# A new order of products and vector work in a fused convolution and SwiGLU kernel

## The chip, the cores and the metric

The kernel runs on one core of a Trainium2 chip. The metric is the time of one execution on the device in microseconds (us). A core has a matrix engine (TensorE, PE in the profile, which writes only to the eight banks of PSUM), a vector engine (VectorE, DVE), a scalar engine (ScalarE, ACT), GpSimd (POOL, which works on SBUF only here) and SyncE (SP), which issues the DMAs. Each engine takes its instructions in the order of the program, and waits where one needs what another engine has not finished yet.

## The reference

The input x has 8 sequences of 4096 tokens of 192 channels. First comes a causal convolution of 7 taps in each channel, with taps that are a softmax over the 7 weights of the channel's head (8 heads of 24 channels):

```python
w = np.exp(weight - np.max(weight, axis=-1, keepdims=True))
w = w / (np.sum(w, axis=-1, keepdims=True) + 1e-09)
out = np.einsum('hk,bskhg->bshg', w, x_unf)      # x_unf: the 7 last tokens of each token
```

Then a SwiGLU block without bias on all 32768 tokens, with d_ff = 1536:

```python
rms = np.sqrt(np.mean(x * x, axis=-1, keepdims=True) + 1e-06)
xn = x / rms * rms_g
g = xn @ w_gate
silu = g * (1.0 / (1.0 + np.exp(-g)))
val = xn @ w_val
return (silu * val @ w_out).astype(np.float32)
```

## The kernel before, in words

**Pairs.** The tokens are worked on in 32 "pairs" of 1024 tokens, that is two groups of 512. Pair 0 is done in a plain way and overlaps the start of the kernel. Pairs 1 to 31 run through the class `Pair` (L821) and take nearly all of the time. A pair has two stages on TensorE: a product stage, which makes gate and value and from them the hidden activations, and an output stage, which multiplies these with w_out.

**Product stage.** The 1536 hidden columns are cut into 4 units of 3 x 128. A unit is a block product: 2 groups of tokens, 3 blocks of inner length 64 (192 = 3 x 64) and 3 blocks of columns, so 6 outputs, numbered v = 0 to 5. In place of 18 block products it makes 15, of sums of inputs (`XSUM`, made once a pair) and sums of weights (`WSUM`, made once). The 15 results are added up in PSUM so that most serve several outputs. `CHAIN` (L713) lists them in order as (v, i): product i is added to the bank that stands for v. `product` (L746) issues one; every product is issued twice, for half 0 (the gate, partitions 0 to 63) and half 1 (the value, partitions 64 to 127). The two halves run side by side in the matrix engine, and every matmul in fp32 leaves two records in the trace. A half has four PSUM banks, handed out from a list of free ones (`free`, `pick`).

**Vector steps.** `Unit.do` (L754) has the steps that go with the products. A name such as `AS41.0.1` in `ORDER` is: the engine (V = VectorE, A = ScalarE, G = GpSimd), the step, the half and the unit.
- S copies a bank to a tile in SBUF (S40, S41, S42, S44: four states of bank 4, as it grows; S00 and S51: banks 0 and 5).
- F ("fork") copies a bank into a new one, from which another output goes on: `FORK` (L717) says that output 0 starts from bank 1, output 2 from bank 4 and output 3 from the negative of bank 5. The fork of bank 4, F2, is made in two parts: F2a, columns 0 to 319 on ScalarE, then F2b, columns 320 to 511 on VectorE (`CUT`, L720).
- C, D and R add a snapshot to a bank, or take it off; R also ends an output and frees its bank. G is the silu of the gate, M the product with the value; G4 and M4 free bank 4.

**Output stage.** It makes a two-by-two block product with seven products in place of eight (`OUTS`), in 84 steps of `tile` (L879). Its sums of activations (S1 to S4 followed by a block number; names with one number after the point) are GpSimd's. In the same time the vector engines prepare later pairs: `cv` are the taps of the convolution for the pair after next, `sq`, `red`, `pow`, `bc`, `mul` its norm, `X0` to `X10` the sums of inputs for the next pair (X10 is the last to touch the input that the next pair's second product (1,4) reads), `fetA`, `fetB`, `load`, `place` and `st` are DMAs, and C22, C21, T22, T21, T12, T11 the last sums and transposes of the output.

**What sets the order.** `ORDER` (L90) is a table that stands in the program. "p2" means: issue two steps of TensorE's line. Everything else is issued where it stands, and a trailing "-" says that the step belongs to the pair before. The order within each engine is therefore that of the table, and where a step stands against the "p" entries also decides which value of a bank it sees, and so who waits for whom. TensorE's own line comes from `products` (L857). Products of a unit before: (4,11), (1,4), (5,6), (4,9), (0,8), (5,13), (4,5), (1,10), (0,3), (4,7), (5,2), (4,12), (2,1), (3,14), (4,0). A product on bank 4 must wait until the snapshot or the fork of the state before it has been read.

Of the kernel before, what the change touches and what calls it, by code (L numbers as in the profile page):

```python
# [19 lines left out]
def kernel(  # L20
# [22 lines left out]
    T = 512  # L43
# [9 lines left out]
    NU = FC // NF  # L53
# [34 lines left out]

    SPAN = 1509
    ORDER = (  # L90
        "p2 Dst1- VT11- p2 AS40.1.0 VS40.0.0 p2 AF0.1.0 GX7- AF0.0.0 Dst0- p2 VC.0.0 Dload-",
        "GX4- p2 VC.1.0 AS41.0.0 VS41.1.0 p2 AS00.1.0 AS00.0.0 p2 VD5.1.0 p2 Vbc- VD5.0.0",
        "AS42.0.0 Gmul- AS42.1.0 p2 AS51.1.0 VR1.1.0 AS51.0.0 p2 VR1.0.0 p2 AF2a.0.0 VF2b.0.0",
        "AF2a.1.0 VF2b.1.0 AG1.0.0 VR0.0.0 p2 VR0.1.0 AF3.0.0 p2 VS44.0.0 AF3.1.0 Dplace- p1",
        "AS44.1.0 VR5.0.0 p1 AG0.0.0 VR5.1.0 p1 AG5.0.0 p1 GM0.1.0 VR3.0.0 p1 AG4.0.0 p1",
        "VR3.1.0 AG3.0.0 GM1.1.0 p1 VR2.1.0 p1 AS40.0.1 VR2.0.0 p1 AS40.1.1 GM5.1.0 p1",
        "VM4.1.0 AF0.0.1 p1 AF0.1.1 VC.0.1 p1 AG2.0.0 p1 VC.1.1 p1 AS41.1.1 GM2.1.0 VS41.0.1",
        "p2 VS00.0.1 AS00.1.1 p1 GM3.1.0 VD5.0.1 p2 VD5.1.1 AS42.0.1 p1 GS3.1 AS42.1.1 p1",
        "VR1.0.1 p1 AS51.0.1 AS51.1.1 p1 VR1.1.1 p1 AG1.0.1 VR0.0.1 p1 AF2a.0.1 GM1.1.1 p1",
        "VF2b.0.1 AF2a.1.1 VF2b.1.1 AG0.0.1 p1 VR0.1.1 p1 AF3.0.1 GS3.0 VF3.1.1 p1 AS44.0.1",  # L100
        "p1 AS44.1.1 VR5.0.1 p1 GS1.0 p1 VR5.1.1 AG5.0.1 p2 VR2.0.1 GM0.1.1 p1 VR2.1.1",
        "AG4.0.1 p1 VR3.1.1 AG2.0.1 p1 GM5.1.1 p1 VR3.0.1 AS40.0.2 p1 AS40.1.2 VM4.1.1 p1",
        "GM2.1.1 AF0.0.2 p1 AF0.1.2 VC.0.2 p1 GS3.2 p1 VC.1.2 p1 AS41.1.2 VS41.0.2 p2",
        "VS00.0.2 GS1.2 AS00.1.2 p1 AG3.0.1 p1 VD5.1.2 GM3.1.1 p1 AS42.0.2 p1 VD5.0.2",
        "AS42.1.2 p1 VR1.0.2 p1 AS51.0.2 GS1.1 AS51.1.2 p1 VR1.1.2 p1 AG1.0.2 VR0.0.2 p1",
        "GS2.1 AF2a.0.2 p1 VF2b.0.2 AF2a.1.2 VF2b.1.2 p1 VR0.1.2 AF3.0.2 p1 GS2.0 VF3.1.2 p1",
        "AS44.0.2 p1 AS44.1.2 VR5.0.2 GM1.1.2 p2 VR5.1.2 AG5.0.2 p2 VR2.0.2 AG0.0.2 GM5.1.2",
        "p1 VR2.1.2 AG2.0.2 p1 VR3.1.2 AG4.0.2 p1 GS2.2 p1 AS40.0.3 VR3.0.2 AS40.1.3 p1",
        "VM4.1.2 p1 GM0.1.2 AF0.0.3 p1 AF0.1.3 VC.0.3 p1 AG3.0.2 GS4.2 p1 VC.1.3 p1 AS41.1.3",
        "VS41.0.3 p1 AS00.0.3 GM3.1.2 p1 VS00.1.3 p2 VD5.0.3 GS3.3 p1 VD5.1.3 AS42.0.3 p1",  # L110
        "AS42.1.3 p1 VR1.0.3 p1 AS51.0.3 GS1.3 AS51.1.3 p1 VR1.1.3 p1 AG1.0.3 VR0.1.3 p1",
        "AF2a.0.3 GM1.1.3 p1 VF2b.0.3 AF2a.1.3 VF2b.1.3 p1 VR0.0.3 p1 GM2.1.2 VF3.1.3 AF3.0.3",
        "p2 AS44.0.3 AS44.1.3 p1 VR5.0.3 GS3.4 p1 VR2.0.3 p1 AG5.0.3 p1 VR5.1.3 GS2.3 AG4.0.3",
        "p2 Acv0_2 VM4.1.3 p1 AG0.0.3 p1 VR3.0.3 p1 GS3.5 DfetA p1 VR3.1.3 AG3.0.3 p1 Vcv1_2",
        "p1 Acv0_1 p1 GM3.1.3 AG2.0.3 VR2.1.3 p2 Acv0_0 p2 GS1.4 Ac1 Vcv1_0 p3 VM0.1.3 p2",
        "VM5.1.3 p2 Vcv1_1 p1 GS1.5 p2 Vcv2_1 p2 Vcv2_2 GS2.5 As7 DfetB p2 Vcv2_0 p2 GS2.4",
        "Vcv3_1 p2 Vcv3_2 p2 VX3 p2 GS4.3 Vcv4_1 p2 Vcv5_1 p2 GS4.4 Vcv3_0 p2 Vcv4_2 p1 GS4.0",
        "p1 Ac2 Vcv4_0 p2 Vcv6_1 p1 GM2.1.3 p4 VX0 p1 GS4.5 Vcv5_0 p3 Vcv6_0 p1 GS4.1 p1",
        "Vcv5_2 p3 Vcv6_2 GX9 p2 VC22 Asq p2 VX1 p2 GX2 VT22 p2 Vred p2 GX6 p3 GX5 p1 VC21 p3",
        "VX8 p2 GX10 VT21 p2 VT12 p1 Gpow p3",  # L120
    )

    cst = ctx.enter_context(tc.tile_pool(name="cst", bufs=1))
# [569 lines left out]
    def put(at, do):  # L693
        heapq.heappush(line, (at, next(tick), do))
# [5 lines left out]
    def plus(s):  # L700
        return ALU.add if s > 0 else ALU.subtract
# [3 lines left out]
    def copy(eng, dst, src, s=1):  # L705
        if eng == "A":
            nc.scalar.activation(out=dst, in_=src, func=AF.Copy, scale=float(s))  # L707
        elif s < 0:
            nc.vector.tensor_scalar(out=dst, in0=src, scalar1=-1.0, scalar2=None, op0=ALU.mult)
        else:  # L710
            nc.vector.tensor_copy(out=dst, in_=src)  # L711

    CHAIN = (  # L713
        (4, 11), (1, 4), (5, 6), (4, 9), (0, 8), (5, 13), (4, 5), (1, 10), (0, 3), (4, 7),
        (5, 2), (4, 12), (2, 1), (3, 14), (4, 0),
    )
    FORK = {0: (1, 1), 2: (4, 1), 3: (5, -1)}  # L717
    RESULT = {1: ("42", -1), 0: ("41", -1), 2: ("51", -1), 5: ("44", -1), 3: ("c", 1)}

    CUT = 320  # L720

    class Unit:
        def __init__(self, u):
# [30 lines left out]
        def do(self, eng, act, h):  # L754
            tl, kind, v = self.tl, act[0], int(act[1:2] or 0)
            if kind == "S":
                t = tl[act[1:], h] = tiles.pop(0)
                copy(eng, t[:], self.old(v, h))
            elif kind == "F":
                src, s = FORK[v]  # L760
                cols = {"a": slice(0, CUT), "b": slice(CUT, T)}.get(act[2:], slice(0, T))
                dst = self.old(v, h) if (v, h) in self.bk else self.new(v, h)
                copy(eng, dst[:, cols], self.old(src, h)[:, cols], s)
            elif kind == "D":
                b, t = self.old(5, h), tl.pop(("00", h))
                nc.vector.tensor_tensor(out=b, in0=b, in1=t[:], op=ALU.add)
                tiles.append(t)
            elif kind == "C":
                t = tl["c", h] = tl.pop(("40", h))
                nc.vector.tensor_tensor(out=t[:], in0=self.old(5, h), in1=t[:], op=ALU.add)  # L770
            elif kind == "R":
                k, s = RESULT[v]
                t = tl.pop((k, h))
                nc.vector.tensor_tensor(  # L774
                    out=self.hv(v) if h else t[:], in0=self.old(v, h), in1=t[:], op=plus(s)
                )
                self.leave(v, h)
                if h:
                    tiles.append(t)
                else:  # L780
                    tl["g", v] = t
            elif kind == "G":
                if v in RESULT:
                    t = src = tl["g", v]
                else:
                    t, src = tiles.pop(0), self.old(v, 0)
                nc.scalar.activation(out=t[:], in_=src[:], func=AF.Silu)  # L787
                if v not in RESULT:
                    self.leave(v, 0)
                tl["g", v] = t  # L790
            else:
                t = tl.pop(("g", v))
                src = self.hv(v) if v in RESULT else self.old(v, 1)
                engine[eng].tensor_tensor(out=self.hv(v), in0=src, in1=t[:], op=ALU.mult)  # L794
                if v not in RESULT:
                    self.leave(v, 1)
                tiles.append(t)
# [23 lines left out]
    class Pair:  # L821
# [33 lines left out]
            free[h].append(i)  # L855

        def products(self):  # L857
            for u in self.units:
                for v, i in CHAIN:
                    for h in range(2):  # L860
                        u.product(h, v, i)
                        yield
            for form, b, lo, hi in OUTS:
                first = form in (1, 7)
                if first:
                    self.open(b, False)
                for k in range(lo, hi):
                    src, right = self.left(form, k), RIGHT[form][:, k]
                    fresh = first and k == 0
                    wide = src.rearrange("p (b q e) -> p q b e", q=2, e=Q)  # L870
                    slim = src.rearrange("p (b q e) -> p q b e", q=NQ, e=Q)
                    for i in range(NQ):
                        self.tile(b, i, 0, 2 * P, right[:, i // 2], wide[:, i % 2], fresh)
                    yield
                    for i in range(NQ):
                        self.tile(b, i, 2 * P, P, right[:, 2], slim[:, i], False)
                    yield
# [87 lines left out]
    def plain(hts):  # L965
# [27 lines left out]
        def values():  # L993
            for u, g, f in groups:
# [7 lines left out]
                yield  # L1002

        return products(), silus(), values()

    LAG = 138
# [116 lines left out]
    p, sl, v = plain(hts)  # L1123
# [31 lines left out]
    c = base + 200  # L1155
# [17 lines left out]
    for p in range(1, PAIRS + 1):  # L1173
        now = Pair(p) if p < PAIRS else None
        for w in order:
# [5 lines left out]
            eng, name = w[0], w[1:]  # L1181
# [34 lines left out]
```

## Time and profile before

| | |
|---|---|
| median of 3 runs | 2668.94 us (2662.84 to 2669.16) |
| profiled execution, span | 2663.6 us |
| matmuls of the product stage (L748) | 7440 records |
| matmuls of the output stage (L880) | 20832 records |
| first part of the fork on ScalarE, 128x320 | 248, mean 423 ns |
| second part on VectorE, 128x192 | 248, mean 366 ns |
| whole copy of a bank to a bank on ScalarE, 128x512 | 403, mean 585 ns |
| whole copy of a bank to SBUF on ScalarE, 128x512 | 1209, mean 597 to 598 ns |
| convolution tap on VectorE (L446), bank to bank | 435, mean 749 ns |
| input sums on VectorE (L669), from the inputs alone | 94, mean 1422 ns |

How to read it: the records of the product stage lie two side by side, one for each half, so their durations must not be added up; the distance from one start to the next tells how fast TensorE goes. A matmul's end is modelled, and matmuls overlap, so a share of 99% busy does not mean that nothing is lost. VectorE and ScalarE overlap their instructions a little too: from start to start they take some 0.08 us less than the duration of one. The chain of waits follows the work that ended last backwards, and shows on which engine time passes that nobody else could hide. A window table gives the busy time of each engine in a stretch; the share of the idle rest on an engine which is not the bound costs nothing.

### The profile page before, as it was taken

What the parts mean: (1) busy time and instruction counts of PE and PEld (TensorE: products, weight loads), DVE (VectorE), ACT (ScalarE), POOL (GpSimd) and SP (SyncE); (2) the same over time, 40 slices, a digit from 0 to 9 for tenths busy, and PEclk for the clock granted to TensorE, in tenths of its full rate; (3) what the DMA queues carried; (4) which work ended last, traced back from release to release, by engine and by line L of the source; (5) the groups of instructions that cost most, each with busy time, mean ns of one, the idle gap of its engine ahead of it and who ended that gap; (6) DMA issues with size and microseconds to landing.
All of it is one profiled execution on the core that took longest, in us unless ns stands there. A gap on an engine that the chain in (4) does not pass through costs nothing.

```text
span 2663.6 us, 71444 instructions
## 1 busy us (share of the span) xinstructions
PE 2623.9 (99%) x29002; PEld 1594.7 (60%) x29002; DVE 2321.4 (87%) x3793; ACT 1562.4 (59%) x2933; POOL 2188.7 (82%) x1785
## 2 busy tenths in 40 slices
PE   6999999999999999999999999999999999999999
PEld 4666666566665556565566565665655656655665
DVE  8988889888889888888888898888988888988865
ACT  5365555765556755556655566555566555676554
POOL 3988889887888888897888888888988888888877
PEclk9999999999999999999999999999999999999999
DMA  6312331323312223213233222233132332122210
GB/s 141 59 35 55 62 55 33 62 38 62 62 38 49 49 51 62 55 33 61 38 62 62 43 44 50 50 62 59 33 58 38 62 62 49 38 54 45 49 37 14
DMA packets 510663, 138.05 MB, mean 52 GB/s; under 512 B 482300, under 2 KB 484860, under 8 KB 510205
## 3 DMA queue, kind: packets, MB, share of 16 engines
q1 hardware_dynamic: 509772, 133.44, 26.5%
q8 instruction: 227, 3.72, 0.6%
q14 instruction: 104, 0.85, 0.1%
q10 hardware_dynamic: 560, 0.03, 0.0%
HBM read 83.87 MB, written 49.55 MB: 50 GB/s over the span
## 4 chain that ended last, share of the span: by engine, by line
PE 94%; DVE 2%; POOL 1%; DMA 1%; SPq 1%; issue 1%; ACT 1%; DVEq 0%; POOLq 0%
PE ps L748 61%; PE ps L880 32%; PE ps L979 1%; POOL wf L351 1%; ACT ps L707 0%; DVE ps L711 0%; SPq L219 0%; SPq L1117 0%; DMA x<-in_x_dram 0%; DMA xh<-in_x_dram 0%; POOL wo_sb L313 0%; DMA ht<-in_moe_w_gate_dram 0%; DMA ht<-in_moe_w_val_dram 0%; DVE xc L669 0%; DVE ht L996 0%
## 5 line engine op out<-in xcount | busy, mean ns | idle before, releaser
L748 PE MATMUL ps<-xc,wf 64*128 64x512 f32 x4960 | 1308.4, 596 | 2.6 <-DVE xc L669 0.9
L748 PEld LDWEIGHTS ps<-xc,wf 64*128 64x128 f32 x4960 | 619.2, 186 | 547.8 <-issue 376.2
L748 PE MATMUL ps<-xb,wf 64*128 64x512 f32 x2480 | 738.2, 591 | 0.0
L707 ACT ACTIVATE tile<-ps 128x512 f32<-128x512 f32 (+1 forms) x703 | 396.4, 593 | 339.9 <-PE ps L748 194.6
L707 ACT ACTIVATE tls<-ps 128x512 f32<-128x512 f32 (+1 forms) x568 | 326.0, 592 | 339.3 <-PE ps L748 198.0
L794 POOL TENSOR_TENSOR ht<-ht,tile 128x512 f32<-128x512 f32 x310 | 391.7, 1274 | 110.5 <-ACT tile L787 110.5
L748 PEld LDWEIGHTS ps<-xb,wf 64*128 64x128 f32 x2480 | 319.8, 187 | 232.2 <-issue 192.7
L707 ACT ACTIVATE ps<-ps 128x512 f32<-128x512 f32 x682 | 343.0, 521 | 91.5 <-PE ps L748 25.2
L794 POOL TENSOR_TENSOR ht<-ht,tls 128x512 f32<-128x512 f32 x248 | 314.3, 1274 | 95.8 <-ACT tls L787 95.8
L908 POOL TENSOR_TENSOR early<-ht 128x512 f32<-128x512 f32 x279 | 354.1, 1274 | 34.2 <-DVE ht L794 26.9
L446 DVE SCALAR_TENSOR_TENSOR ps<-xh,tp,ps 128x512 f32<-128x512 f32 x435 | 307.4, 749 | 18.2 <-ACT ps L438 16.2
L880 PE MATMUL ps<-ht,wo_sb 128*32 128x256 f32 (+1 forms) x6944 | 309.9, 326 | 0.0
L908 POOL TENSOR_TENSOR ht<-ht 128x512 f32<-128x512 f32 x186 | 238.4, 1282 | 49.1 <-DVE ht L794 36.9
L880 PEld LDWEIGHTS ps<-ht,wo_sb 128*32 128x32 f32 x6944 | 218.0, 110 | 91.2 <-issue 23.5
L774 DVE TENSOR_TENSOR tile<-ps,tile 128x512 f32<-128x512 f32 x341 | 232.0, 683 | 21.6 <-PE ps L748 10.1
L880 PE MATMUL ps<-ht,x 128*32 128x256 f32 (+1 forms) x5952 | 249.6, 326 | 0.2 <-issue 0.2
L774 DVE TENSOR_TENSOR ht<-ps,tile 128x512 f32<-128x512 f32 x357 | 241.6, 681 | 7.4 <-ACT tile L707 7.4
L880 PEld LDWEIGHTS ps<-ht,x 128*32 128x32 f32 x5952 | 194.4, 110 | 49.6 <-issue 0.3
L787 ACT ACTIVATE tile<-tile 128x512 f32<-128x512 f32 x341 | 212.5, 629 | 17.6 <-DVE tile L774 16.8
L774 DVE TENSOR_TENSOR tls<-ps,tls 128x512 f32<-128x512 f32 x279 | 189.9, 684 | 21.8 <-PE ps L748 10.4
L880 PE MATMUL ps<-early,x 128*32 128x256 f32 (+1 forms) x4464 | 193.9, 326 | 0.0
L774 DVE TENSOR_TENSOR ht<-ps,tls 128x512 f32<-128x512 f32 x263 | 177.9, 681 | 8.2 <-ACT tls L707 8.2
(130 smaller groups left out, 3297.8 us busy)
## 6 DMA issues: line engine op xcount, KB each, us to landing
xb<-xd SPq DMA_DIRECT2D x124, 384.0 KB
xd<-yn SPq DMA_DIRECT2D x248, 96.0 KB
out_dram<-o_sb SPq DMA_DIRECT2D x186, 128.0 KB
xh<-in_x_dram SPq DMA_DIRECT2D x192, 105.0 KB
xh<-in_x_dram SPq DMA_DIRECT2D x56, 98.4 KB
ht<-in_moe_w_gate_dram SPq DMA_DIRECT2D x12, 192.0 KB
ht<-in_moe_w_val_dram SPq DMA_DIRECT2D x12, 192.0 KB
tls<-in_moe_w_out_dram SPq DMA_DIRECT2D x8, 192.0 KB
```

Of the source, the lines that this page charges most:

```text
L351: nc.gpsimd.tensor_tensor(out=t[:, d, :], in0=t[:, a, :], in1=t[:, b, :], op=ALU.add if op == "add" else ALU.subtract,)
L446: nc.vector.scalar_tensor_tensor(out=dst, in0=xk, scalar=w, in1=at, op0=ALU.mult, op1=ALU.add)
L707: nc.scalar.activation(out=dst, in_=src, func=AF.Copy, scale=float(s))
L748: nc.tensor.matmul(out=self.new(v, h, True) if first else self.old(v, h), lhsT=wf[self.u][HALF[h], WAT[i], :], rhs=x_op(XOP[i])[HALF[h]], ...
L774: nc.vector.tensor_tensor(out=self.hv(v) if h else t[:], in0=self.old(v, h), in1=t[:], op=plus(s))
L787: nc.scalar.activation(out=t[:], in_=src[:], func=AF.Silu)
L794: engine[eng].tensor_tensor(out=self.hv(v), in0=src, in1=t[:], op=ALU.mult)
L880: nc.tensor.matmul(out=self.bank(b)[i * Q : (i + 1) * Q, at : at + n], lhsT=left, rhs=cols, start=fresh, stop=True, skip_group_check=True, ...
L908: engine[eng].tensor_tensor(out=dst, in0=a, in1=b, op=op)
L979: nc.tensor.matmul(out=bank(h, bks[h])[:], lhsT=wf[u][HALF[h], k * NF + f, :], rhs=xb[HALF[h], g, k, :], start=(k == 0), stop=(k == KP - 1 ...
```

## The change

There are three parts.

1. The products of neighbouring units are interlaced: the last product of a unit on bank 4, (4,0), is issued after the first product of the next unit, (4,11). (4,9) goes ahead of (5,6), (4,5) ahead of (5,13), (4,7) ahead of (0,3), and (4,12) behind (2,1). It is meant to leave two other products between any two on bank 4, which leaves the snapshot or fork more time. Unit 0 and unit 3 have rows of their own, since unit 0 has no unit before it and unit 3 none after it in the pair.
2. The fork of bank 4 becomes one copy (F2) on ScalarE. `CUT` goes.
3. `ORDER` is written anew for all engines: some snapshots and forks, multiplications and input sums change their engine, and nearly all change their place. X10, X2 and X5 go from GpSimd to VectorE, X1 and X3 the other way; T21 goes from the end of the output stage into unit 0 of the next pair.

```diff
     SPAN = 1509
     ORDER = (
-        "p2 Dst1- VT11- p2 AS40.1.0 VS40.0.0 p2 AF0.1.0 GX7- AF0.0.0 Dst0- p2 VC.0.0 Dload-",
...
-        "AF2a.1.0 VF2b.1.0 AG1.0.0 VR0.0.0 p2 VR0.1.0 AF3.0.0 p2 VS44.0.0 AF3.1.0 Dplace- p1",
...
-        "Vcv5_2 p3 Vcv6_2 GX9 p2 VC22 Asq p2 VX1 p2 GX2 VT22 p2 Vred p2 GX6 p3 GX5 p1 VC21 p3",
-        "VX8 p2 GX10 VT21 p2 VT12 p1 Gpow p3",
+        "p2 VT11- p2 AS40.1.0 AS40.0.0 p2 AF0.0.0 GX9- AF0.1.0 Dst0- p2 VC.1.0 Dload- GX4- p2",
+        "Vbc- AS41.0.0 VS41.1.0 VC.0.0 p1 AS00.1.0 p1 Gmul- VT21- AS00.0.0 p2 AS42.0.0",
...
+        "AS40.0.1 VR5.0.0 AS40.1.1 p2 AG4.0.0 VR5.1.0 AG5.0.0 p1 VM4.1.0 p1 AF0.0.1 VF0.1.1",
...
+        "AS51.1.1 p2 VR1.1.1 AF2.0.1 p1 GS1.0 p1 AF2.1.1 VR0.0.1 AG1.0.1 p1 VR0.1.1 p1",
...
+        "Vcv5_1 p2 Vcv6_0 p1 GM2.1.3 p1 Vcv6_2 p3 GX7 p3 GX3 p2 VC22 p2 Vcv6_1 p2 VT22 Asq p2",
+        "VX2 p2 GS4.5 VC21 p1 Vred p2 GX6 p5 VX5 p2 VX8 p2 VX10 p1 Gpow VT12 p2",
     )
...
     CHAIN = (
-        (4, 11), (1, 4), (5, 6), (4, 9), (0, 8), (5, 13), (4, 5), (1, 10), (0, 3), (4, 7),
-        (5, 2), (4, 12), (2, 1), (3, 14), (4, 0),
+        (1, 4), (4, 9), (5, 6), (0, 8), (4, 5), (5, 13), (1, 10), (4, 7), (0, 3), (5, 2),
+        (2, 1), (4, 12), (3, 14),
     )
+    CHAINS = [
+        [(u, 4, 11)] + [(u - 1, 4, 0)] * (u > 0) + [(u, *c) for c in CHAIN] for u in range(NU)
+    ]
+    CHAINS[0][2:4] = CHAINS[0][3:1:-1]
+    CHAINS[-1][-3:] = [(NU - 1, 4, 12), (NU - 1, 2, 1), (NU - 1, 3, 14), (NU - 1, 4, 0)]
...
-    CUT = 320
...
             elif kind == "F":
                 src, s = FORK[v]
-                cols = {"a": slice(0, CUT), "b": slice(CUT, T)}.get(act[2:], slice(0, T))
-                dst = self.old(v, h) if (v, h) in self.bk else self.new(v, h)
-                copy(eng, dst[:, cols], self.old(src, h)[:, cols], s)
+                copy(eng, self.new(v, h), self.old(src, h), s)
...
         def products(self):
-            for u in self.units:
-                for v, i in CHAIN:
-                    for h in range(2):
-                        u.product(h, v, i)
-                        yield
+            for u, v, i in itertools.chain(*CHAINS):
+                for h in range(2):
+                    self.units[u].product(h, v, i)
+                    yield
```

## The prediction

> **What bounds the kernel now.** I read the page's busy shares first, then the chain of waits in order of time, then the timeline around its one break, then busy time by stage.
>
> ```profile
> PE 2623.9 (99%) x29002; PEld 1594.7 (60%) x29002; DVE 2321.4 (87%) x3793; ACT 1562.4 (59%) x2933; POOL 2188.7 (82%) x1785
> ```
>
> TensorE is said to be busy 99% of the span, so only what goes on inside its stream can be gained. The chain shows one pair (eleventh of 31 alike):
>
> ```profile
> 1036.26 8.83 PE ps L748 x40
> 1045.10 0.41 ACT ps L707
> 1045.51 0.02 issue
> 1045.53 0.38 DVE ps L711
> 1045.91 0.04 issue
> 1045.95 43.75 PE ps L748 x192
> 1089.70 27.44 PE ps L880 x672
> ```
>
> It leaves TensorE at one place, for the two parts of the fork (ACT's 320 columns, then DVE's 192). How far this is from an unbroken stream is read from a quiet stretch and from the stage as a whole:
>
> ```profile
> 1038.87 3.60 PE L748 MATMUL ps<-xc,wf 64*128 64x512 f32 x16
> 1042.30 1.88 PE L748 MATMUL ps<-xb,wf 64*128 64x512 f32 x8
> ```
> ```profile
> core 0: us, PE busy (x) PEld busy (x) DVE busy (x) ACT busy (x) POOL busy (x), PEclk, DMA share, GB/s
> 1036.19:1089.54 53.35, 53.30 (x244) 27.53 (x240) 45.92 (x79) 41.84 (x81) 43.11 (x36) 1.00 0.28 47
> 1089.54:1117.06 27.52, 27.52 (x673) 20.03 (x672) 26.02 (x40) 6.82 (x11) 24.94 (x20) 1.00 0.26 60
> ```
>
> From 1038.87 to 1042.30, 16 records start: four products, since each has two halves side by side and two records a half. So a product takes 3.43/4 = 0.858 us, and the 60 products of a pair 51.5 us. The stage takes 53.35: 1.84 us too much, though "busy" hides it. The output stage has no such excess (672 records without a break). The break itself:
>
> ```profile
> 1044.02 3.38 PE L748 MATMUL ps<-xc,wf 64*128 64x512 f32 x12
> 1045.08 0.75 ACT L707 ACTIVATE ps<-ps 128x320 f32<-128x320 f32 x2 [0.45 <-PE ps L748]
> 1045.53 0.70 DVE L711 COPY ps<-ps 128x192 f32<-128x192 f32 x2 [0.56 <-ACT ps L707]
> 1045.95 1.05 PEld L748 LDWEIGHTS ps<-xc,wf 64*128 64x128 f32 x6 [0.88 <-DVE ps L711]
> ```
>
> Product (4,7) starts at 1044.02, and (4,12) is due two products later, 1044.02 + 1.717 = 1045.74. The fork sees (4,7) at 1045.08, 1.06 after its start. Half 0 is through at 1045.90 and half 1 at 1046.23 (1045.53 + 0.70); with 0.05 for the hand-back TensorE goes on at 1045.95 and 1046.28, 0.21 and 0.54 late. Each restart costs 0.10 more (a first record of 0.69 against 0.59). In units 1 to 3 the halves are already staggered, and both come 0.32 late (sum of start-to-start gaps over 0.429 at this product). Half 1 loses 0.65 + 3 x 0.32 + 0.10 = 1.71 us a pair; the rest, 0.13, is the ramp at the pair's start, which stays. The list of waits agrees on the culprit:
>
> ```profile
> PEld ps L748 <- DVE ps L711: 81.2, 213, 1.1
> PEld ps L748 <- ACT ps L707: 35.6, 156, 0.4
> ```
>
> **What the Trainium skill says.** (1) "PSUM — Partial Sum Buffer", section "PSUM bank collisions raise a hardware error": two engines may not touch the same bank and quadrant at once, reads included. That is why the fork's two parts stand in line: DVE begins 0.03 after ACT's end at 1045.50, so splitting one bank over two engines never halves its time. (2) "TensorE: Matmul & The Clock Gate", section "The mechanism": matmuls start and end in program order, only weight loads are pulled ahead. So a product that waits holds all behind it. The trace agrees: no later product starts before 1045.95. (3) "SBUF — State Buffer", section "Who interferes with whom": a DVE instruction with two SBUF inputs and a GpSimd instruction that reads SBUF exclude each other. The trace agrees: DVE's input sum takes 0.68 where it comes first (GpSimd's power beside it then takes 2.20 in place of 1.65) and 1.19 to 1.75 where GpSimd was there before.
>
> **The change, part by part.**
> *Spacing.* Next unit's (4,11) is moved ahead of (4,0), (4,12) behind (2,1). Between two products on bank 4 lie now at least two others: a budget of 3 x 0.858 = 2.575 us in place of 1.717. A fork as one ACT copy (0.585) needs 1.06 + 0.585 + 0.05 = 1.70 for half 0; half 1 follows on ACT 0.49 later (start to start of two such copies): 2.19. Both fit with 0.38 spare. The same sum covers the snapshots S40, S41, S42, S44 (0.597 each): 2.21 of 2.575. So 1.71 us a pair go.
> *Exception.* Unit 0 has no earlier unit to interlace: (4,9) stands at place 3, (4,5) at 5. Budget 1.717; S41 half 0 on ACT needs 1.06 + 0.597 + 0.05 = 1.71, half 1 on DVE (0.683 to 0.691) 1.80. Cost 0.08, with a restart up to 0.18.
> *Banks.* Each half has four banks; with two units open a product often takes a bank just given back. By hand over a middle unit (time 0 at (4,11), a product at place k visible at 0.858k + 1.06, DVE 0.60 from start to start, ACT 0.50; "due" is 0.858k less the hand-back of 0.05): R3 ends 1.48, (1,4) due 1.66. G4, behind S40 on ACT, ends 2.69; M4 follows on DVE and ends 3.40, (5,6) on half 1 due 3.38: 0.02 late. C ends 5.8, (5,13) due 5.96. D5 twice, then R1 twice: R1.1 ends 9.55, F2.1 takes its bank and ends 10.17, (2,1) due 10.25: the thinnest, 0.08. R0.1 10.93, F3.1 11.72, due 11.97. R2.1 12.65, next (4,11) due 12.83. Three units at 0.02: 0.06 a pair.
> *Work moved.* DVE loses eight fork parts (8 x 0.366) and six whole copies (0.68), gains three F0, two S42, two multiplications with both inputs in SBUF (0.68 to 0.86) and one input sum: about 1 us less. ACT gets 1 to 2 us more, but has 42 of 53 busy. GpSimd loses three of 1.27. None of it is the bound; counted as 0.
> *End of the output stage.* X10 moves from GpSimd to DVE's last place, and the second product of the next pair, (1,4), reads it. Before:
>
> ```profile
> 1111.78 1.70 DVE L472 TENSOR_REDUCE s<-yn 128x64 f32<-128x1536 f32 x1
> ...
> 1114.40 1.19 DVE L669 TENSOR_TENSOR xc<-xb 128x512 f32<-128x512 f32 x1
> ...
> 1115.73 1.65 POOL L481 TENSOR_TENSOR r<-r,nhalf 128x8 f32<-128x8 f32 x1
> ```
>
> DVE after step 60 of the output stage (19.75 us in): C22, cv6_1, T22, X2, C21 take about 3.0 us, the reduction and its two followers 2.15, X5 and X8 0.6 each, X10 0.68: end at 26.8, due at 28.3. If GpSimd's power (1.65) gets in between X8 and X10 it ends at 28.4; if X2 also waits for a GpSimd sum, at 29.0. So 0 to 0.7 us a pair. I take 0.15, as most orders of arrival fit.
> *Sum.* 1.71 - 0.08 - 0.06 - 0.15 = 1.42 us a pair, 31 pairs: 44 us. 2668.9 - 44 = 2625. The output stage's rare breaks (seven in 31 pairs, some 7 us, no releaser) stay.
>
> **Rivals.**
> *A, DVE's tail sets the pair's start:* 0.7 lost, 0.8 x 31 = 25 gained, 2644. For it: DVE is 95% busy in the output stage (26.02 of 27.52), and X0 now needs inputs that land some 13 us in. Against: C22 can't start before step 60, so earlier lateness is absorbed.
> *B, a wait on a bank takes the fork's place:* margins of 0.02 to 0.2 us are smaller than one displaced instruction of 0.6. At 0.35 in each of four units all is given back: 2668. Against: R1 and R0 already hand banks to forks before, without waits but the fork's own.
> *C, slower:* A and B together, with DVE's queue falling behind in every unit (18 instructions of 0.60 fill 11 of 12.9 us): 1.4 + 0.7 lost against 1.4 gained, 2690.
> *D, all goes and nothing comes:* 1.71 x 31 = 53, 2616.
>
> **How the numbers follow.** Forecast (2618 to 2635) 0.60, A (2636 to 2655) 0.19, B (2656 to 2676) 0.09, C 0.05, D 0.07. The three times before differ by 6 us, which widens each. The range 2613 to 2650 leaves out B, C and the end of A. Faster by over 0.3% (under 2661): forecast, A, D and a quarter of B, 0.88; within 0.3%: 0.06; slower: 0.06.
>
> **What would show it.** Right: product stage of 51.8 to 52.0 us, no copy of 192 columns, the chain runs from output stage to output stage on TensorE alone, (4,12) never late. In unit 0 a gap under 0.2 at (4,5). Wrong: gaps at (1,4) of the pair's start with X10 ending last (A), or at (2,1), (5,6), (5,13) behind R1, M4, C (B). If the gaps at the fork went and the products ran further apart than 0.858, my rate would be wrong.

## The result and the profile after

The changed kernel takes 2641.11 us (median of 4 runs, 2638.08 to 2642.31) against 2668.29 us: a ratio of 0.9901, with a 95% interval of 0.9884 to 0.9918. It is faster by 27 us, inside the stated range, where 44 were forecast. The product stage did what was forecast. The start of a pair gave 18 us of it back.

The stages of two pairs that follow each other, in the window table of the changed kernel (the stretches are product stage, output stage with the gap behind it, and both again):

```profile
core 0: us, PE busy (x) PEld busy (x) DVE busy (x) ACT busy (x) POOL busy (x), PEclk, DMA share, GB/s
1184.50:1236.45 51.95, 51.95 (x240) 37.38 (x240) 44.56 (x74) 43.76 (x82) 39.96 (x34) 1.00 0.29 48
1236.53:1264.93 28.40, 27.51 (x673) 19.96 (x673) 25.58 (x40) 6.52 (x11) 24.86 (x20) 1.00 0.26 59
1264.94:1316.88 51.94, 51.94 (x240) 37.34 (x240) 44.55 (x74) 43.75 (x82) 39.85 (x33) 1.00 0.29 48
1316.97:1344.40 27.43, 27.43 (x673) 20.01 (x672) 24.49 (x39) 6.51 (x11) 24.95 (x19) 1.00 0.28 62
```

The product stage is at 51.94 us in place of 53.35. The output stages differ: with TensorE busy for nearly the same time (27.51 and 27.43), the first is 0.97 longer than the second. In the trace 18 of the 30 changes from pair to pair have this gap of about 1.17 us between the last output step and the next product, where before all had 0.20; eight still have 0.20, and four lie at 0.32 to 0.47. Together it is 18.0 us (sum of the gaps less 0.20). The chain of waits over the same two pairs:

```profile
1184.50 52.10 PE ps L749 x240
1236.60 19.68 PE ps L878 x480
...
1256.38 0.56 DVE tile L924
...
1257.59 0.55 DVE o_sb L893 x2
1258.14 0.14 DVE xc L667
1258.28 1.40 issue
1259.69 0.54 DVE tls L924
1260.23 1.67 DVE s L470
...
1262.42 0.66 DVE xc L667 x2
...
1263.54 0.69 DVE xc L667
1264.23 0.57 DVE o_sb L893 x2
1264.80 0.14 issue
1264.93 52.10 PE ps L749 x240
1317.04 27.44 PE ps L878 x672
```

Inside the product stage the chain is now one piece of TensorE, with no fork in it. But 8.7 us ahead of the late pair it leaves TensorE and runs down VectorE's whole tail, from C22 (L924 at 1256.38) over X2 (L667 at 1258.14) to T12 (the last transposes, L893); the 1.40 us of "issue" lie within X2's own time. The second pair has none of this. Now VectorE's timeline in both tails; first the late one:

```profile
1257.51 0.63 DVE L893 STREAM_TRANSPOSE o_sb<-tile 128x256 f32<-128x256 f32 x2
1258.06 1.70 DVE L667 TENSOR_TENSOR xc<-xb,xc 128x512 f32<-128x512 f32 x1
1259.69 0.54 DVE L924 TENSOR_TENSOR tls<-ps,tls 128x384 f32<-128x384 f32 x1
```
```profile
1337.94 0.63 DVE L893 STREAM_TRANSPOSE o_sb<-tile 128x256 f32<-128x256 f32 x2
1338.49 0.71 DVE L667 TENSOR_TENSOR xc<-xb,xc 128x512 f32<-128x512 f32 x1
1339.13 0.55 DVE L924 TENSOR_TENSOR tls<-ps,tls 128x384 f32<-128x384 f32 x1
```

and GpSimd beside it, in the same two tails (X6 is the line of L667):

```profile
1256.69 1.28 POOL L906 TENSOR_TENSOR tls<-ht,nt 128x512 f32<-128x512 f32 x1
1257.92 1.29 POOL L667 TENSOR_TENSOR xc<-xb,xc 128x512 f32<-128x512 f32 x1
```
```profile
1337.37 1.29 POOL L906 TENSOR_TENSOR tls<-ht,nt 128x512 f32<-128x512 f32 x1
1338.61 1.73 POOL L667 TENSOR_TENSOR xc<-xb,xc 128x512 f32<-128x512 f32 x1
```

In the late tail X6 begins 0.14 us ahead of X2, and X2 takes 1.70: until X6 ends at 1259.21, then 0.55 more. In the punctual one X2 begins 0.12 ahead of X6; X2 takes 0.71, and it is X6 that takes 1.73. Neither reads what the other writes (X2 adds an input and X0's sum, X6 an input and X3's, by `XSUM`), so this is no wait for data. The mean of the group hides that there are two kinds of X2. Over all pairs X2 begins 21.53 us into an unbroken output stage, and X6 at 21.37 to 21.44 or at 21.60 to 21.65. Which of the two goes back to the inputs: where the second half of the next pair's input lands 13.15 us into the stage or earlier, X6 is the early one, where it lands at 13.55 or later, X0 begins later, GpSimd's queue slips by 0.2, and X6 comes second. A late DMA goes with a punctual pair. (Pairs with a break in TensorE's own stream shift X2 too and fall outside this rule.)

### The profile page after: what moved, and what is told of

Read it like the earlier page. It is cut to its first block, busy times and chain, and to the rows that moved or that the text cites. A ratio compares the mean times of both kernels' runs of the same rounds, so it can differ in the third digit from the quotient of the medians.

```text
span 2636.2 us, 71036 instructions
## 1 busy us (share of the span) xinstructions
PE 2581.8 (98%) x29002; PEld 1878.4 (71%) x29002; DVE 2271.7 (86%) x3606; ACT 1614.4 (61%) x2964; POOL 2091.1 (79%) x1693
## 4 chain that ended last, share of the span: by engine, by line
PE 89%; DVE 6%; issue 2%; POOL 1%; SPq 1%; DMA 1%; ACT 0%; DVEq 0%; POOLq 0%
PE ps L749 61%; PE ps L878 27%; DVE xc L667 1%; DVE s L470 1%; DVE o_sb L893 1%; PE ps L977 1%; POOL wf L349 1%; DVE tls L924 1%; DVE y L444 0%; SPq L1115 0%; DMA x<-in_x_dram 0%; DVE y L405 0%; POOL wo_sb L311 0%; SPq L217 0%; DMA ht<-in_moe_w_val_dram 0%
## 5 line engine op out<-in xcount | busy, mean ns | idle before, releaser
L749 PE MATMUL ps<-xc,wf 64*128 64x512 f32 x4960 | 1249.7, 592 | 17.3 <-DVE o_sb L893 16.3
L749 PEld LDWEIGHTS ps<-xc,wf 64*128 64x128 f32 x4960 | 764.2, 186 | 319.5 <-issue 117.3
L749 PE MATMUL ps<-xb,wf 64*128 64x512 f32 x2480 | 707.7, 589 | 0.0
L705 ACT ACTIVATE tls<-ps 128x512 f32<-128x512 f32 (+1 forms) x636 | 365.6, 589 | 384.7 <-PE ps L878 204.0
L705 ACT ACTIVATE tile<-ps 128x512 f32<-128x512 f32 x697 | 400.0, 594 | 277.2 <-PE ps L749 166.9
L749 PEld LDWEIGHTS ps<-xb,wf 64*128 64x128 f32 x2480 | 394.7, 187 | 138.4 <-issue 38.1
L705 ACT ACTIVATE ps<-ps 128x512 f32<-128x512 f32 (+1 forms) x651 | 366.9, 578 | 53.1 <-PE ps L878 38.8
L793 POOL TENSOR_TENSOR ht<-ht,tls 128x512 f32<-128x512 f32 x201 | 254.9, 1275 | 72.4 <-ACT tls L786 70.5
L878 PEld LDWEIGHTS ps<-ht,x 128*32 128x32 f32 x5952 | 191.7, 110 | 52.1 <-issue 0.7
L773 DVE TENSOR_TENSOR ht<-ps,tls 128x512 f32<-128x512 f32 x311 | 212.0, 682 | 0.0
L773 DVE TENSOR_TENSOR ht<-ps,tile 128x512 f32<-128x512 f32 x309 | 210.5, 681 | 0.0
```

The source lines that it names most:

```text
L749: nc.tensor.matmul(out=self.new(v, h, True) if first else self.old(v, h), lhsT=wf[self.u][HALF[h], WAT[i], :], rhs=x_op(XOP[i])[HALF[h]], ...
L773: nc.vector.tensor_tensor(out=self.hv(v) if h else t[:], in0=self.old(v, h), in1=t[:], op=plus(s))
L878: nc.tensor.matmul(out=self.bank(b)[i * Q : (i + 1) * Q, at : at + n], lhsT=left, rhs=cols, start=fresh, stop=True, skip_group_check=True, ...
```

## Experiments

Theory P: X2 meets X6 at the SBUF port, T12 behind it is late, and the first product (4,11) waits for the bank that T12 gives back. The other question was what the two parts of the change are worth alone.

**X2 ahead of C22**, where VectorE stands idle waiting for TensorE.

```diff
-... p3 GX7 p3 GX3 p2 VC22 ...
-"VX2 p2 GS4.5 VC21 ...
+... p3 GX7 p3 GX3 VX2 p2 VC22 ...
+"p2 GS4.5 VC21 ...
```

> The changed kernel with X2 put ahead of C22 in VectorE's queue, where VectorE waits for TensorE anyway; nothing else moves. Theory P (port): the 0.97 us lost ahead of (4,11) in 18 of 30 changes of pair comes from X2, which finds GpSimd's X6 at work on SBUF and takes 1.70 in place of 0.71; all behind it on VectorE, T12 too, is late, and (4,11) takes the bank that T12 gives back. Then with X2 out of this place no pair starts late: gap between output stage and next product 0.20 in nearly all, 2641 - 17 = 2624 us. Rival Q (the queue is too long with X10 in it, X2 or not): X2 takes its 0.6 out of the tail, so the late pairs stay late by 0.3 to 0.4: 2630. Rival N (T12 is not what (4,11) waits for): 2641.

2624.51 us; ratio to the kernel before 0.9835, interval 0.9821 to 0.985. The gap is 0.20 in 29 of 30 changes of pair. Two pairs in the chain of waits:

```profile
by line: PE ps L749 66.0%; PE ps L878 34.3%
...
783.64 52.06 PE ps L749 x240
835.71 27.44 PE ps L878 x672
863.15 52.06 PE ps L749 x240
915.21 27.44 PE ps L878 x672
```

VectorE is gone from it. Rival Q asked for 2630 and late pairs, N for 2641: both fall. X2 still meets a sum of GpSimd there (X2 takes 0.83 or 1.05, and X7 or X3 beside it 1.73 in place of 1.28), but ahead of C22 VectorE has the time. It is 17 us under the change, and no other kernel here is faster.

**T12 ahead of X8.**

```diff
-... p5 VX5 p2 VX8 p2 VX10 p1 Gpow VT12 p2
+... p5 VX5 p2 VT12 VX8 p2 VX10 p1 Gpow p2
```

> The changed kernel with T12 put ahead of X8 and X10 in VectorE's queue. Theory P and rival Q both say that T12 then ends 1.2 us earlier, before the output stage is over, so (4,11) no longer waits; X2 still takes 1.70 in the same share of pairs. X10 ends 0.6 later than now, about 0.9 us into the next pair, where (1,4) reads it: a gap of 0 to 0.1 there in those pairs. 2641 - 17 = 2624, up to 2627. Rival N (something else than the bank that T12 gives back): the gaps stay, 2641. Rival X (X10 is as urgent as T12): the gap moves to (1,4), 0.5 or more there, 2633 to 2641.

2626.09 us; ratio 0.984 (0.9825 to 0.9855). All 30 gaps are 0.20, although the port is fought for as before, and X10 ends later than it did. No gap appears at (1,4): X10 ends at most 0.82 into the pair, and (1,4) starts at 0.96. So the next product waits for T12's bank, and X10, which the prediction had named as the one with the deadline, has room. The cure at the cause and the cure at the deadline are worth the same.

This run also shows GpSimd's power, which the prediction let hold VectorE for 1.65 us. It begins ahead of X8 and X10 here:

```profile
780.55 0.65 DVE L667 TENSOR_TENSOR xc<-xb 128x512 f32<-128x512 f32 x1
781.12 0.68 DVE L667 TENSOR_TENSOR xc<-xc 128x512 f32<-128x512 f32 x1
```
```profile
780.01 1.65 POOL L479 TENSOR_TENSOR r<-r,nhalf 128x8 f32<-128x8 f32 x1
```

X8 and X10 take no longer than without the power beside them, and the power no longer than without them: a power that begins 0.54 us ahead of X8 (0.34 in most pairs) does not hold VectorE up.

**X6 left out.**

```diff
-... p1 Vred p2 GX6 p5 VX5 ...
+... p1 Vred p7 VX5 ...
```

> The changed kernel without X6: one of the eleven input sums of the next pair is left out, so a product uses an older sum; nothing else is changed. Theory P (port): nothing on GpSimd reads SBUF when X2 comes, X2 takes 0.7 in all pairs and no pair starts late: gaps of 0.20, about 2622 us. Rival Q (the tail of VectorE's queue is too long, X2 only rides on it): VectorE's queue has the same instructions as before, so the late pairs stay late by 0.97.

The product that needs X6 takes an older sum here, so this kernel leaves out a part of the reference's work, one instruction a pair. One execution, 2629.64 us. X2 takes 0.65 to 0.72 in all pairs but the last, and all gaps are 0.20. VectorE's queue is the same as in the change, so the length of that queue is not the cause; Q falls a second time. (The time is above the forecast 2622 since TensorE's own breaks in the output stage add up to 10.4 us in this execution, against 4.2 in the change's. They carry no releaser in any kernel here, the one before included.)

**X2 behind C21.**

```diff
-"VX2 p2 GS4.5 VC21 p1 Vred ...
+"p2 GS4.5 VC21 VX2 p1 Vred ...
```

> The changed kernel with X2 behind C21 in place of ahead of it, so that X2 comes half a us later, when X6 surely has begun. Theory P: X2 waits for X6 in all pairs (1.1 to 1.3 in place of 0.71 or 1.70) and ends where it ends in the late pairs now; C21 is through by then, so the reduction begins 0.5 earlier than in a late pair and 0.5 later than in a punctual one. Every pair starts late by 0.4 to 0.55, with no two kinds of pair: 30 x 0.5 = 15 against 18 x 0.97 = 17.5 now, 2637 to 2642 us. Rival R (what parts late from punctual pairs is something else, for instance the DMA's landing, and not what X2 meets): still two kinds, 0.2 and about 1.2.

2637.98 us; ratio 0.9887 (0.9872 to 0.9902). All pairs are late now, as P had it, but against its "no two kinds" there are still different ones: most gaps are 0.62 to 0.75 (0.5 late, as forecast), six are 0.92 to 0.96, and three about 0.4. The expectation missed that X6 itself begins at two times, 0.2 apart, and X2 takes 0.91 to 1.00 in most pairs (1.1 to 1.3 expected). X2 ends about 0.55 after X6 in either case:

```profile
778.87 0.56 DVE L924 TENSOR_TENSOR tls<-ps,tls 128x384 f32<-128x384 f32 x1 [0.19 <-PE ps L878]
779.35 0.97 DVE L667 TENSOR_TENSOR xc<-xb,xc 128x512 f32<-128x512 f32 x1
```
```profile
778.47 1.29 POOL L667 TENSOR_TENSOR xc<-xb,xc 128x512 f32<-128x512 f32 x1
```

X6 ends at 779.76, X2 at 780.32. The pairs with a late landing, punctual in the change, are the latest here (X2 1.20, gap 0.94). So landing time alone does not make a pair late; what X2 meets does.

**The whole copy of the fork alone, both halves on ScalarE**, in the kernel before, with its old order of products:

```diff
-... p2 AF2a.0.0 VF2b.0.0 AF2a.1.0 VF2b.1.0 AG1.0.0 ...
+... p2 AF2.0.0 AF2.1.0 AG1.0.0 ...
```

> The kernel before with one edit: the fork of bank 4 is one copy a half, both on ScalarE, in the old order of products; this is part 2 of the change alone. Theory F: half 1 is copied 0.49 after half 0, so it is 0.47 late in unit 0, with 0.10 for the restart; from then on half 1 runs that much behind half 0, and its copy comes just after half 0's without a further wait. Product stage 52.2, 2668 - 31 x 1.1 = 2634. Rival S (spacing is what counts): 0.47 or more in each of four units, as much as before or more, 2665 to 2680.

2639.62 us; ratio 0.9891 (0.9876 to 0.9906), as good as the whole change. Product stage:

```profile
785.50:837.93 52.43, 52.43 (x244) 28.54 (x240) 43.43 (x71) 42.59 (x81) 42.83 (x36) 1.00 0.28 47
```

With the restart, half 1 is 0.50 late in unit 0 (0.57 forecast), and then not in time, but only 0.1 late in each of units 1 to 3. The sum 1.70 of 1.717 us leaves a margin of 0.02; that the stagger between the halves uses it up is a reading and was not tested. So theory F holds but for 0.2 us in the stage (and 6 us in the time, 2634 forecast), and the rival's 2665 does not.

**The same with half 1 on VectorE.**

```diff
+... p2 AF2.0.0 VF2.1.0 AG1.0.0 ...
```

> The kernel before with one edit: the fork of bank 4 is one copy a half, half 0 on ScalarE and half 1 on VectorE, in the old order of products (two places between (4,7) and (4,12)). Theory F (the fork in two parts was the cost, not the spacing): 1.06 + 0.585 + 0.05 = 1.70 on ScalarE fits in 1.717, 1.06 + 0.69 + 0.05 = 1.80 on VectorE is 0.08 late once, with 0.10 for the restart, and then half 1 runs staggered and is in time in the later units. Product stage 51.8 to 51.9, 2668 - 31 x 1.5 = 2622. Rival S (a fork needs three places, as the change assumes): gaps of 0.1 to 0.3 in every unit, product stage 52.3 to 53.0, 2640 to 2658.

2643.67 us; ratio 0.9905 (0.9888 to 0.9921), and a product stage of 52.58: inside the rival's range, not in mine. Half 1, whose copy takes 0.70 on VectorE, loses 0.23 at (4,12) in unit 0 and again 0.1 to 0.2 in every later unit, restarts included. Here two engines side by side bring no more than ScalarE alone with one copy after the other.

**The spacing alone**: the change with its fork in two parts again. The new order of the vector work stays in, so this is parts 1 and 3 of the change.

```diff
-... VR1.1.0 AF2.0.0 p2 AF2.1.0 VR0.0.0 ...
+... VR1.1.0 AF2a.0.0 VF2b.0.0 p2 AF2a.1.0 VF2b.1.0 VR0.0.0 ...
```

> The changed kernel with the fork of bank 4 again in two parts (320 columns on ScalarE, 192 on VectorE), in the new order of products: part 1 of the change without part 2. Theory F2 (spacing and whole copy are two ways to the same gain): the split fork of half 0 needs 1.93 and that of half 1 2.3 of the 2.575 there are, but VectorE's part stands behind R1 in its queue (ends about 10.4, due 10.25), so 0.15 late and 0.10 for the restart in one or more units: product stage 52.1 to 52.6, 2645 to 2662 us. Rival (the spacing does all, the form of the fork nothing): 51.94, 2641. Rival (the spacing does nothing without the whole copy): 53.3, 2680.

2665.26 us; ratio 0.9991 (0.9985 to 0.9998): nearly nothing, and just beyond what was forecast (stage 52.1 to 52.6, 2645 to 2662 us). Product stage, and VectorE in the middle of a unit 0:

```profile
953.38:1006.06 52.68, 52.68 (x240) 35.45 (x240) 46.20 (x82) 42.45 (x82) 39.87 (x33) 1.00 0.28 47
```
```profile
962.38 0.37 DVE L709 COPY ps<-ps 128x192 f32<-128x192 f32 x1
962.98 0.37 DVE L709 COPY ps<-ps 128x192 f32<-128x192 f32 x1 [0.23 <-ACT ps L705]
963.25 0.68 DVE L775 TENSOR_TENSOR tile<-ps,tile 128x512 f32<-128x512 f32 x1
963.85 0.68 DVE L775 TENSOR_TENSOR ht<-ps,tls 128x512 f32<-128x512 f32 x1
```

VectorE waits 0.23 for ScalarE's part, with R0 behind it in its queue, and then runs for 2.7 us without a pause. TensorE is late at other products than in the change: 0.35 at (2,1) of unit 0, where it was 0.12, about 0.1 at (4,12) and (3,14) of unit 1, and 0.24 at the end of unit 3. The stage still wins 0.67 over the one before, and the late pairs (18 of 30, 15.6 us) take most of that back.

**Both repairs together.**

> The changed kernel with X2 ahead of C22 and T12 ahead of X8. With either repair the gap ahead of the first product is gone, so both together should add nothing: 2622 to 2627 us, product stage 51.97, gaps 0.20. If it is faster than 2620, something else in the start of a pair was late.

2624.96 us; ratio 0.9838 (0.9823 to 0.9852); product stage 51.97, all gaps 0.20. As expected, nothing is added.

## Why the prediction was right, and where it was off

- *Where the loss was.* Right: 1.84 us a pair between the ideal 51.5 and 53.35, nearly all at the fork, though TensorE was "99% busy". With the waits gone the stage is at 51.94, within the forecast 51.8 to 52.0.
- *Spacing and fork, -1.71.* Right together. Taken apart, the whole copy alone brings 0.92 of the stage's 1.41 and the spacing alone 0.67. The prediction said that three places are needed for the fork; the sum it gave for one half (1.70 against the 1.717 of two places) already said that the copy almost fits without them, and this was not followed up. The split fork was the dearer fault: the whole copy is worth 0.92 us a stage in the old order and 0.74 in the new, the new order 0.67 with the split fork and 0.49 with the whole copy.
- *Exception in unit 0, 0.08 to 0.18.* Right place, (4,9) to (4,5), size 0.21 to 0.25 in the sum with its restart, and 0.11 later at half 1 of (2,1). Half 0 too starts only 0.07 after VectorE's copy of half 1 ends, 0.14 after its own copy on ScalarE. Why it does not go at once stays open.
- *Banks, 0.06.* Less: delays of 0.01 at most in units 1 to 3. The hand-made table of a unit held.
- *Work moved, 0.* Right for the product stage: ScalarE is busy for 43.8 of 51.9 us and nothing waits for that.
- *End of the output stage, 0.15.* This term was mis-sized: 0.60 on average (18.0 / 30). The mechanism was in the prediction ("if X2 also waits for a GpSimd sum"), as were 0.7 us for it and rival A's 2644. That the 0.7 comes so near to the 0.97 of a late pair is luck: it was made of a power that holds VectorE for 1.6 and of 0.6 for X2, where the power cost nothing and X2 about 1.0. Three things were wrong. X2 was treated as a matter of chance, where the trace of before, with its X1, X3 and X8 of 0.8 to 1.75 us beside GpSimd, gave reason to look where X6 would start (that a table of GpSimd's queue would have found it within 0.1 us of X2 was not tried). The power was taken to hold VectorE up; in the runs it held up nothing. And the deadline was laid on X10, "DVE's last place", read by (1,4), when `ORDER` has T12 behind it, and T12's deadline, (4,11), comes first: `pick` gives a product first the banks that the output stage has used, and in half 0 that is the bank of its result X, which T12 gives back.
- *The sum.* 1.41 x 31 = 44 gained in the products, 18 lost at the starts, and about 3 us fewer breaks of TensorE's own in this execution (4.2 against 7.1): 29, close to the 27.4 between the two profiled spans. The time lies in rival A's band (2636 to 2655, given 0.19), not in the forecast's own (2618 to 2635), and only the range around both held. Forecast and rival A were both half right: the forecast in the stage, A in the place that takes back, though A's sign, a gap at (1,4) with X10 last, did not appear; the gap stands at (4,11). With the repair the forecast's 2625 is reached (2624.5).

The Trainium skill's page "SBUF — State Buffer", section "Who interferes with whom", says of VectorE and GpSimd that issue order decides who blocks. X2 and X6 show both orders in one execution: 1.70 and 1.29, or 0.71 and 1.73.

## What to carry to other kernels

A busy matrix engine is checked against its own quiet stretches: count the records in a stretch without waits, and multiply. When a tight order of instructions is rewritten, follow each engine's last instructions across the stage's end, and ask which buffer the first instruction of the next stage takes, not only which data. Where an instruction of two SBUF inputs on VectorE can meet GpSimd work within a tenth of a us, move it into a place where VectorE waits anyway; and before reordering products around a copy in two parts, try the single copy alone.

## What the runs showed of the hardware that was not expected

- A stage can come in two kinds within one execution because two queues race for the SBUF port: which comes first turns on some 0.1 us, and costs 1.0 us.
- A later landing of an input went with an earlier start of the next pair: GpSimd's X6 slipped by 0.2 us, and VectorE's X2 went first.
- A tiny GpSimd instruction can be held up too, but held nobody up in these runs. The power on 128 x 8 elements took 1.97 us where X8 had begun before it in the change, and 1.65 in most pairs of the kernel before (2.20 in four pairs, beside X8). Where it began 0.34 ahead of X8 (T12 ahead of X8) it took 1.65, and X8 and X10 beside it kept their 0.65 and 0.68. So the prediction's "exclude each other" does not hold for the power's whole length.
- A matmul that has waited is slow to start: its first record lasts 0.66 to 0.69 in place of 0.59 us, and 0.08 to 0.10 is lost on top of the wait each time.
